# Weight row ends issued by the GpSimd queue in transfers of 8 x 4 rows, with values three groups behind the keys

## The chip, the cores and the metric

The kernel runs on one core of a Trainium2 chip. The metric is the device time of one execution in microseconds. Eleven executions of the kernel before lie between 195.41 and 195.97 us, 0.3% apart, so differences of one per cent are read from several rounds, in which the kernel in question and the kernel before run in turn on the same chip. A profile is one execution. Its span is shorter than the device time (198.4 us for an execution of 200.14 us).

## The reference, cut to what matters

It is one decode step: eight batch rows of attention over a cached window of 1024 positions, and a small MLP, mixed by a gate.

```python
B, Sq, D = 8, 1, 448; Hq, Hkv, Sk, Dh = 16, 8, 4096, 256; F = 1792
q = (x @ wq)                      # wq: 448 x 4096
k, v = last 1024 positions of the caches, 8 kv heads, 8 batches
o = softmax(q k^T / 16) v
a = o @ wo                        # wo: 4096 x 448
b = gelu(layernorm(x) @ w1 + b1) @ w2 + b2     # w1: 448 x 1792
out = g * a + (1 - g) * b         # g = sigmoid(x . gate_w)
```

Keys and values of the window are 67 MB in bf16, the weights 10.6 MB. All of it is read once. The width 448 is 3 x 128 + 64, so `wq` and `w1` have 64 rows left over after three full sets of 128 partitions. These 64 rows are the "row ends" of this document.

## The kernel before

Everything large goes through a ring of nine slots of 128 partitions x 16 KB, filled in a fixed order by one queue, SP (SyncE). One load of a key or value group (four heads of one batch) is 2 MB: 16 KB for each of 128 partitions.

```python
wq_m = A_wq[0:DM, :].rearrange("(p r) n -> p (r n)", r=NR)     # DM = 384, NR = 3
wq_t = A_wq[DM:D, :].rearrange("r (h n) -> (r h) n", h=2)      # 64 rows as 128 half rows
w1_t = B_w1[DM:D, :].rearrange("r (h n) -> (r h) n", h=2)
...
add_kv("k", A_k_cache, 0, parts=2)
add(("w1",), rows_loader([w1_m, w1_t]))
add(("wq", 0), rows_loader([wq_m[:, 0 : 2 * HD]]))
add(("wq", 1), rows_loader([wq_m[:, 2 * HD : 3 * HD], wq_t]))
add(("w2",), rows_loader([w2_v]))
for u in range(1, NQ - 1):                 # NQ = 16 groups
    add_kv("k", A_k_cache, u)
    if u < NQ - 2:
        add_kv("v", A_v_cache, u - 1)
add_kv("k", A_k_cache, NQ - 1)
for u in range(NQ - 3, NQ):
    add_kv("v", A_v_cache, u)
... then wo, in pieces of 896, 896, 896, 448, 224 and 224 KB
```

Each row end is split in two halves, so that all 128 partitions take the same share. The price is a second set of transposed activations and some more matmuls. At the end, values 14 and 15 and the output projection follow the last keys:

```python
u = NQ - 1
transpose_keys(u, steps(u - 1)); scores(u); top(u)
values(u - 2); finish(u - 2)
expo(u); turn(u); bring(u)
values(u - 1); ...; finish(u - 1)
spread_rows(0, HALF); values(u); finish(u); project(0); ...
```

## Time and profile before

| | before |
|---|---|
| time, median (range) of three executions | 195.52 us (195.46 to 195.59) |
| span of the profile | 193.7 us |
| read from HBM | 77.68 MB |
| rate while loading | about 425 GB/s |
| last matmul ends | 190.43 us |
| last weight piece landed | 189.82 us |

From the page of the kernel before: the busy share of the 16 DMA engines in 40 slices of 4.84 us (9 is 90% or more), what they moved in each slice, and two of the queues with packets, MB and share of the engines' time.

```profile
DMA  5999999999999999999999999999999999999950
GB/s 203 397 437 415 430 431 428 426 426 416 420 423 430 426 426 423 430 430 423 425 423 423 430 423 416 428 430 420 426 426 430 420 433 420 423 433 404 414 217 10
...
q1 hardware_dynamic: 6512, 77.67, 95.3%
q8 instruction: 18, 0.29, 0.6%
```

The load runs from the second slice to the 38th without a gap. From the same page, the chain of work that ended last:

```profile
DMA 82%; PE 9%; ACT 3%; DVE 2%; issue 1%; SPq 1%; ACTq 0%
```

The engines are named as the profiler names them: PE is TensorE (matmuls; PEld are its weight loads), DVE is VectorE, ACT is ScalarE, POOL is GpSimd. "SPq" and "ACTq" are the queues of SyncE and ScalarE. Two neighbouring pieces of the same chain, in order of time (start, duration, what):

```profile
120.98 39.72 DMA slot<-in_A_k_cache_dram
...
160.74 0.64 PE ktp L322 x8
```

So the kernel is bound by the load until 160.7 us, when key group 14 has landed. From there a compute chain is the last one. The end of it in the timeline of the kernel before (start, duration, engine, line, operation, output and inputs, count):

```profile
187.11 0.92 PE L563 MATMUL A_ps<-slot,oP 128*8 128x112 bf16 x32
...
187.97 2.46 PE L563 MATMUL A_ps<-slot,oP 128*8 128x112 bf16 x96
...
190.48 0.33 DVE L580 SCALAR_TENSOR_TENSOR res<-A_ps,gg_s,mixb 128x112 bf16<-128x112 f32 x1 [1.92 <-PE A_ps L563]
```

The 96 matmuls run without a wait for the load. But the load ends only about half a microsecond before them (0.6 us by the table, 0.4 us on the clock of the views), so both have to shorten for the time to fall.

One more reading is needed. For each transfer of the bulk load the trace keeps 16 semaphore increments, which I read as one for each of the 16 DMA engines, when its part has landed. They do not name the engine, but the distances to the first repeat from transfer to transfer (15 of the 16 in the two transfers below, within 0.01 us), so each can be followed. Two transfers of the kernel before: time of the first landing, then the distance of all 16 to it, in us.

```
43.69 | 0.00 0.06 0.07 0.10 0.13 0.14 0.18 0.39 0.48 0.62 0.64 0.92 1.07 1.75 1.93 2.01
48.59 | 0.00 0.06 0.07 0.10 0.13 0.14 0.17 0.39 0.48 0.62 0.64 1.07 1.75 1.93 2.02 2.48
last transfer:
184.96 | 0.00 0.08 0.17 0.40 0.49 0.62 0.83 2.04 3.17 3.20 3.22 3.49 3.56 3.75 4.02 4.86
```

Between the first two rows the engine at 0.92 went to 2.48, and no other moved. At 44.72 a packet of 16 KB of the instruction queue ran for 1.02 us. By my matching, the others between 18 and 186 us go with such steps in the same way: each sets one engine back by about 1.55 us, and eight engines take turns. The packets do not name their engine, so this is a reading of the landings. At the end eight engines are late, and the slowest of them ends the load: it lands 2.7 us after the mean of the 16 (187.08).

### The profile page before, as it was taken

What the parts mean: (1) busy time and instruction counts of PE and PEld (TensorE: products, weight loads), DVE (VectorE), ACT (ScalarE), POOL (GpSimd) and SP (SyncE); (2) the same over time, 40 slices, a digit from 0 to 9 for tenths busy, and PEclk for the clock granted to TensorE, in tenths of its full rate; (3) what the DMA queues carried; (4) which work ended last, traced back from release to release, by engine and by line L of the source; (5) the groups of instructions that cost most, each with busy time, mean ns of one, the idle gap of its engine ahead of it and who ended that gap; (6) DMA issues with size and microseconds to landing.
All of it is one profiled execution on the core that took longest, in us unless ns stands there. A gap on an engine that the chain in (4) does not pass through costs nothing.

```text
span 193.7 us, 5200 instructions
## 1 busy us (share of the span) xinstructions
PE 148.1 (76%) x2334; PEld 110.3 (57%) x2334; DVE 112.9 (58%) x259; ACT 82.7 (43%) x101; POOL 0.8 (0%) x7
## 2 busy tenths in 40 slices
PE   1399967777778787878778787878868787984883
PEld 0399936555464646465637373737464646662672
DVE  7532344757475757584847575757565757786320
ACT  2352004536272728181808282828273636582000
POOL 1000000000000000000000000000000000000000
PEclk9998559999999999999999999999999999999555
DMA  5999999999999999999999999999999999999950
GB/s 203 397 437 415 430 431 428 426 426 416 420 423 430 426 426 423 430 430 423 425 423 423 430 423 416 428 430 420 426 426 430 420 433 420 423 433 404 414 217 10
DMA packets 6744, 78.02 MB, mean 403 GB/s; under 512 B 945, under 2 KB 1346, under 8 KB 1986
## 3 DMA queue, kind: packets, MB, share of 16 engines
q1 hardware_dynamic: 6512, 77.67, 95.3%
q8 instruction: 18, 0.29, 0.6%
q10 hardware_dynamic: 210, 0.02, 0.1%
q14 instruction: 4, 0.03, 0.0%
HBM read 77.68 MB, written 0.01 MB: 401 GB/s over the span
## 4 chain that ended last, share of the span: by engine, by line
DMA 82%; PE 9%; ACT 3%; DVE 2%; issue 1%; SPq 1%; ACTq 0%
DMA slot<-in_A_k_cache_dram 77%; DMA slot<-in_B_w_dram 5%; ACT kt L325 2%; PE S_ps L360 2%; PE ktp L322 2%; PE PO L420 2%; PE A_ps L563 2%; ACT E L380 1%; PE sm L437 1%; SPq L107 1%; DVE EB L388 1%; DVE nmx L372 1%; PE sm L399 0%; PE sm L396 0%; PE pp L547 0%
## 5 line engine op out<-in xcount | busy, mean ns | idle before, releaser
L325 ACT COPY kt<-ktp 128x1024 bf16<-128x1024 bf16 x64 | 63.2, 1017 | 82.2 <-PE ktp L322 82.2
L322 PE MATMUL ktp<-ident,slot 128*128 128x128 bf16 x1024 | 70.2, 224 | 22.1 <-ACT kt L325 11.4
L322 PEld LDWEIGHTS <-slot 128*128 128x128 bf16 x1024 | 63.7, 102 | 29.0 <-issue 15.7
L327 DVE COPY kt<-ktp 128x1024 bf16<-128x1024 bf16 x64 | 41.3, 685 | 15.8 <-PE ktp L322 15.6
L372 DVE TENSOR_REDUCE nmx<-S_ps 128x1 f32<-128x1024 f32 x16 | 19.6, 1225 | 22.3 <-PE S_ps L360 22.3
L360 PE MATMUL S_ps<-kt,qw 128*8 128x512 bf16 x256 | 32.3, 627 | 0.3 <-DVE qw L351 0.3
L388 DVE STREAM_TRANSPOSE EB<-E 128x1024 bf16<-128x1024 bf16 x16 | 19.9, 1245 | 6.7 <-ACT E L380 6.5
L420 PE MATMUL PO<-slot,ET 128*8 128x256 bf16 x512 | 18.5, 290 | 6.4 <-DVE ET L401 6.4
L380 ACT ACTIVATE E<-S_ps,nmx 128x1024 bf16<-128x1024 f32 x16 | 17.9, 1120 | 2.4 <-DVE nmx L373 2.4
L420 PEld LDWEIGHTS <-ET 128*8 128x8 bf16 x512 | 12.2, 90 | 10.5 <-DVE ET L401 8.7
L360 PEld LDWEIGHTS <-qw 128*8 128x8 bf16 x256 | 7.3, 95 | 12.0 <-issue 10.4
L401 DVE CAST ET<-sm 128x256 bf16<-128x256 f32 x16 | 6.7, 417 | 0.7 <-PE sm L399 0.7
L396 PE MATMUL sm<-EB,perm 128*128 128x256 bf16 x16 | 4.5, 280 | 1.6 <-DVE EB L388 1.6
L399 PE MATMUL sm<-selr,ones_f 128*128 128x8 f32 x32 | 5.5, 244 | 0.0
L440 DVE CAST oT<-sm 128x16 bf16<-128x16 f32 x16 | 3.5, 221 | 2.8 <-PE sm L437 2.8
L399 PEld LDWEIGHTS sm<-selr,ones_f 128*128 128x128 f32 x32 | 5.0, 196 | 0.1
L339 PE MATMUL qt<-xT,slot 128*128 128x8 bf16 x128 | 3.6, 168 | 0.4 <-DVE z L470 0.4
L339 PEld LDWEIGHTS <-slot 128*128 128x128 bf16 x128 | 3.6, 104 | 0.4 <-issue 0.3
L470 DVE TENSOR_TENSOR z<-hT,b_sb 128x112 f32<-128x112 f32 x1 | 0.3, 275 | 5.3 <-PE hT L460 5.3
L563 PE MATMUL A_ps<-slot,oP 128*8 128x112 bf16 x128 | 3.3, 294 | 0.0
L380 ACT ACTIVATION_READ_ACCUMULATOR E<-S_ps,nmx 128x1 f32 x16 | 3.2, 202 | 0.0
L403 DVE RECIPROCAL rb<-sm 128x8 f32<-128x8 f32 x16 | 3.2, 199 | 0.0
(122 smaller groups left out, 72.2 us busy)
## 6 DMA issues: line engine op xcount, KB each, us to landing
slot<-in_A_v_cache_dram SPq DMA_DIRECT2D x16, 2048.0 KB, 39.3
slot<-in_A_k_cache_dram SPq DMA_DIRECT2D x15, 2048.0 KB, 39.6
slot<-in_A_wo_dram SPq DMA_DIRECT2D x3, 896.0 KB, 32.0
slot<-in_A_k_cache_dram SPq DMA_DIRECT2D x2, 1024.0 KB, 7.2
slot<-in_A_wq_dram SPq DMA_DIRECT2D x1, 2048.0 KB
slot<-in_B_w_dram SPq DMA_DIRECT2D x1, 1568.0 KB
slot<-in_B_w_dram SPq DMA_DIRECT2D x1, 1344.0 KB, 10.1
slot<-in_A_wq_dram SPq DMA_DIRECT2D x1, 1024.0 KB
```

The costliest lines, as they stand in the source:

```text
L322: nc.tensor.transpose(ktp[:, c, :], kn[:, o : o + P], ident[:])
L325: nc.scalar.copy(dst, ktp[:])
L327: nc.vector.tensor_copy(dst, ktp[:])
L339: nc.tensor.matmul(qt[:, k, :], lhsT=w[:, o + c : o + c + P], rhs=xT[:, r + half, :], start=(r == 0 and k == 0), stop=(r == NR), skip_grou ...
L360: nc.tensor.matmul(S_ps[32 * a : 32 * a + RQ, hf * CH * SK : (hf + 1) * CH * SK], lhsT=qw[:, j, b, half, a, :], rhs=KT[hf][:, j, :, a::QUA ...
L372: nc.vector.reduce_max(nmx[:], S_ps[:], axis=AXIS.X, negate=True)
L380: nc.scalar.activation(E[:], S_ps[:], ACT.Exp, bias=nmx[:], scale=1.0, accum_out=rowsum[:])
L388: nc.vector.transpose(EB[:].rearrange("p c r -> p (c r)"), E[:])
L399: nc.tensor.matmul(sm[:, NCK, :], lhsT=ones_f[:], rhs=selr[:], start=True, stop=True)
L401: nc.vector.tensor_copy(ET[:], sm[:, 0:NCK, :])
L420: nc.tensor.matmul(PO[32 * t : 32 * t + RQ, :], lhsT=ET[:, c, 0:RQ], rhs=vn[:, c * Dh : (c + 1) * Dh], start=(c < QUAD), stop=(c >= NCK - ...
L563: nc.tensor.matmul(dst, lhsT=oP[:, j, q, :], rhs=w[:, o + cols.start : o + cols.stop], start=(q == 0 and j == 0), stop=(q == NHQ - 1 and j ...
```

## The change

The intent, as the diff shows it: the row ends are loaded as 64 full rows on partitions 64 to 127, by the GpSimd queue, so that the SP queue does not carry them, and one set of transposed activations for the row ends is enough in place of two (in the MLP, 14 matmuls for them in place of 28). Each transfer is shaped as 8 x 4 rows. Small dummy transfers ("side") stand between them: 14 rows ahead of the first, eight ahead of each other one, ten after the last. I took them to be there to pick the eight engines that work on the row ends. Values are loaded and used three groups after their keys (before: one).

```diff
+    LAG = 3
+    ER = P - DT                                  # 64
...
+    def step_over(n):
+        ...
+        nc.gpsimd.dma_start(side[0:n, ...], A_wq[0:n, 0:32]...)    # n rows of 64 bytes
+    def ends(t, o, src):
+        n = src.shape[1]
+        for h in range(DT // 32):
+            rows = src[DM + 32 * h : DM + 32 * h + 32, :]
+            step_over(NB if turns[0] else 14)    # NB = 8
+            nc.gpsimd.dma_start(
+                t[ER + 32 * h : ER + 32 * h + 32, o : o + n],
+                rows.rearrange("(j i) n -> i j n", i=NB),
+            )
+            if turns[0] == 4:
+                step_over(10)
...
-    add(("w1",), rows_loader([w1_m, w1_t]))
+    add(("w1",), rows_loader([w1_m], B_w1))      # the second argument goes to ends()
...
-    for u in range(1, NQ - 1):
+    for u in range(1, NQ):
         add_kv("k", A_k_cache, u)
-        if u < NQ - 2:
-            add_kv("v", A_v_cache, u - 1)
+        if u >= LAG:
+            add_kv("v", A_v_cache, u - LAG)
...
-                    lhsT=w[:, o + c : o + c + P],
-                    rhs=xT[:, r + half, :],
+                    lhsT=w[p0:P, c : c + P],     # p0 = 64 for the row ends
+                    rhs=xT[p0:P, r, :],
```

(Cut: the same for `w1`, the pools that hold softmax results longer, the identity matrix built ahead of the loads, and the loop of the values.)

More of the change, by code (lines that the diff above doesn't have):

```diff
@@ L51 @@
     NF = F // P
-    FH = F // 2
-    HH = HD // 2
     QUAD = 4
@@ L76 @@
     ktpool = ctx.enter_context(tc.tile_pool(name="ktpool", bufs=4))
-    epool = ctx.enter_context(tc.tile_pool(name="epool", bufs=3))
+    epool = ctx.enter_context(tc.tile_pool(name="epool", bufs=2))
+    opool = ctx.enter_context(tc.tile_pool(name="opool", bufs=LAG + 1))
     ps_s = ctx.enter_context(tc.tile_pool(name="ps_s", bufs=1, space=PSUM))
@@ L111, in kv_loader, with rows_loader @@
         return load
-    def rows_loader(pieces):
+    side = consts.tile([16, 10, 32], BF16)
+    turns = [0]
+    def step_over(n):
+        i = turns[0]
+        turns[0] += 1
+        nc.gpsimd.dma_start(
+            side[0:n, 2 * i : 2 * i + 2, 0:16],
+            A_wq[0:n, 0:32].rearrange("b (a n) -> b a n", a=2),
+        )
[4 more added lines that the diff above has]
+            step_over(NB if turns[0] else 14)
+            nc.gpsimd.dma_start(
+                t[ER + 32 * h : ER + 32 * h + 32, o : o + n],
+                rows.rearrange("(j i) n -> i j n", i=NB),
+            )
+            if turns[0] == 4:
+                step_over(10)
+    def rows_loader(pieces, tail=None):
         def load(t):
@@ L124, in load @@
                 o += n
+            if tail is not None:
+                ends(t, o, tail)
         return load
@@ L137 @@
     wq_m = A_wq[0:DM, :].rearrange("(p r) n -> p (r n)", r=NR)
-    wq_t = A_wq[DM:D, :].rearrange("r (h n) -> (r h) n", h=2)
     w1_m = B_w1[0:DM, :].rearrange("(p r) f -> p (r f)", r=NR)
-    w1_t = B_w1[DM:D, :].rearrange("r (h n) -> (r h) n", h=2)
     w2_v = B_w2.rearrange("(p c) n -> p (c n)", c=NF)
@@ L144 @@
     add_kv("k", A_k_cache, 0, parts=2)
-    add(("w1",), rows_loader([w1_m, w1_t]))
+    add(("w1",), rows_loader([w1_m], B_w1))
     add(("wq", 0), rows_loader([wq_m[:, 0 : 2 * HD]]))
-    add(("wq", 1), rows_loader([wq_m[:, 2 * HD : 3 * HD], wq_t]))
+    add(("wq", 1), rows_loader([wq_m[:, 2 * HD : 3 * HD]], A_wq))
     add(("w2",), rows_loader([w2_v]))
-    for u in range(1, NQ - 1):
+    for u in range(1, NQ):
         add_kv("k", A_k_cache, u)
-        if u < NQ - 2:
-            add_kv("v", A_v_cache, u - 1)
-    add_kv("k", A_k_cache, NQ - 1)
-    for u in range(NQ - 3, NQ):
+        if u >= LAG:
+            add_kv("v", A_v_cache, u - LAG)
+    for u in range(NQ - LAG, NQ):
         add_kv("v", A_v_cache, u)
@@ L171 @@
     x_sb = consts.tile([NB, D], BF16)
+    ident = consts.tile([P, P], BF16)
+    make_identity(nc, ident[:])
     pump()
@@ L181 @@
     nc.scalar.dma_start(b1_sb[:], B_b1.rearrange("(p c) -> p c", c=NF))
-    ident = consts.tile([P, P], BF16)
-    make_identity(nc, ident[:])
     ones_f = consts.tile([P, P], F32)
@@ L191 @@
     nc.vector.memset(PO[:], 0.0)
-    NX = NR + 2
+    NX = NR + 1
     DQ = D // QUAD
@@ L200, in quads @@
         ]
-    xz = consts.tile([NB, 2, P], BF16)
-    yz = consts.tile([NB, 2, P], BF16)
+    xz = consts.tile([NB, P], BF16)
+    yz = consts.tile([NB, P], BF16)
     nc.vector.memset(xz[:], 0.0)
@@ L223, in transposed, with ends_of @@
             nc.tensor.transpose(tp[:, r, :], src[:, r:DM:NR], ident[:NB, :NB])
-        for h in range(2):
-            nc.tensor.transpose(tp[:, NR + h, :], srcz[:, h, :], ident[:NB, :NB])
+        nc.tensor.transpose(tp[:, NR, :], srcz[:], ident[:NB, :NB])
         nc.vector.tensor_copy(dst[:], tp[:])
-    for h in range(2):
-        nc.vector.tensor_copy(xz[:, h, h::2], x_sb[:, DM:D])
+    def ends_of(dst, src):
+        nc.vector.tensor_copy(
+            dst[:, ER:P].rearrange("b (h i j) -> b h i j", h=DT // 32, i=NB),
+            src[:, DM:D].rearrange("b (h j i) -> b h i j", h=DT // 32, i=NB),
+        )
+    ends_of(xz, x_sb)
     transposed(xT, x_sb, xz)
@@ L270, in norm_and_gate @@
         )
-        for h in range(2):
-            nc.vector.tensor_copy(yz[:, h, h::2], y_sb[:, DM:D])
+        ends_of(yz, y_sb)
         transposed(yT, y_sb, yz)
@@ L335, in query @@
             w, o = slot("wq", r // 2), (r % 2) * HD
+            p0 = ER if r == NR else 0
             for k in range(Hq * NJ):
-                col = (k // NJ) * Dh + (k % NJ) * P
-                half, c = divmod(col, HH) if r == NR else (0, col)
+                c = o + (k // NJ) * Dh + (k % NJ) * P
                 nc.tensor.matmul(
                     qt[:, k, :],
-                    lhsT=w[:, o + c : o + c + P],
-                    rhs=xT[:, r + half, :],
+                    lhsT=w[p0:P, c : c + P],
+                    rhs=xT[p0:P, r, :],
                     start=(r == 0 and k == 0),
@@ L399, in bring @@
         nc.tensor.matmul(sm[:, NCK, :], lhsT=ones_f[:], rhs=selr[:], start=True, stop=True)
-        ET = epool.tile([P, NCK, RQ], BF16, tag="ET", name="ET")
+        ET = opool.tile([P, NCK, RQ], BF16, tag="ET", name="ET")
         nc.vector.tensor_copy(ET[:], sm[:, 0:NCK, :])
@@ L403, in bring @@
         nc.vector.reciprocal(rb[:], sm[:, NCK, :])
-        rsel = epool.tile([P, RQ], F32, tag="rsel", name="rsel")
+        rsel = opool.tile([P, RQ], F32, tag="rsel", name="rsel")
         nc.vector.tensor_tensor(rsel[:], rb[:], sel[:], op=ALU.mult)
@@ L457, in mlp_hidden @@
                 )
-        for h in range(2):
-            for c in range(NF):
-                nc.tensor.matmul(
-                    hT[64 * h : 64 * h + 64, c, :],
-                    lhsT=w[:, NR * F + c : NR * F + FH : NF],
-                    rhs=yT[:, NR + h, :],
-                    start=False,
-                    stop=True,
-                    skip_group_check=True,
-                )
+        for c in range(NF):
+            nc.tensor.matmul(
+                hT[:, c, :],
+                lhsT=w[ER:P, NR * F + c : NR * F + F : NF],
+                rhs=yT[ER:P, NR, :],
+                start=False,
+                stop=True,
+                skip_group_check=True,
+            )
         done()
@@ L518 @@
     mlp_out(hs)
-    for u in range(1, NQ - 1):
+    for u in range(1, NQ):
         transpose_keys(u, steps(u - 1))
-        if u < NQ - 2:
-            values(u - 1)
+        if u >= LAG:
+            values(u - LAG)
         scores(u)
         top(u)
-        if u < NQ - 2:
-            finish(u - 1)
+        if u >= LAG:
+            finish(u - LAG)
     u = NQ - 1
-    transpose_keys(u, steps(u - 1))
-    scores(u)
-    top(u)
+    expo(u)
+    turn(u)
     values(u - 2)
     finish(u - 2)
-    expo(u)
-    turn(u)
     bring(u)
@@ L574 @@
     finish(u)
-    project(0)
     spread_rows(HALF, NHQ)
-    for q in range(1, NHQ):
+    for q in range(NHQ):
         project(q)
```

## The prediction

> **What bounds the kernel now.** The bulk load. The page shows 77.68 MB read at about 425 GB/s, the DMA row at nine tenths nearly throughout. In the chain of waits 82% is DMA, up to the landing of key group 14 (160.7 us). Then a compute chain binds: keys 14 and 15 are transposed back to back (160.7 to 175.1), softmax of 15, values 14, values 15, output projection; its last matmul ends at 190.43. The trace's semaphore increments of the last weight transfer land from 184.96 to 189.82, so both must shorten.
>
> **The 16 DMA engines do not end together.** In the last transfer seven land within 0.83 us, one 2.04 us behind the first, seven 3.2 to 4.0, one 4.9. The mean is 187.08. Following the gaps back, each 16 KB packet of the instruction queue (18 of them, about 10 us apart, 1.1 us each) sets one engine back by 1.55 us; the pattern fits eight engines in turn, two hits each, one three.
>
> **What the change does.**
> 1. Values trail keys by three groups: key 15 lands one 2 MB load (4.9 us) earlier and key 14 two, so no back-to-back transposes wait behind the last keys. Compute is then done with the values near 185, with slack. The end becomes: last weight piece lands, eight matmuls (about 0.2 us), mix 0.33 us, output as before. Alone this gains about 0.4 us.
> 2. The 64 row ends (229 KB and 524 KB) leave the SP queue, where every engine carries 47 KB of them. Each GpSimd transfer has a source of outer size 8[...]. These get 94 KB, the others none: plus and minus 47 KB, 1.77 us at 16 KB per 0.614 us. No run here shows which eight, nor whether the upper partitions slow anyone.
> 3. Fewer MLP matmuls (1.5 us), and the GpSimd issues, are early, off the critical path; the nine slots stay ahead.
>
> **Sum.** If the eight are those that fetch no instructions: fetch engines end 1.4 to 3.1 us after today's first, the others 1.8 to 3.8, last landing near 188.7 in place of 189.8; with slack in compute about 1.3 us saved. If the groups half overlap: nothing. If they coincide: last landing 191.6, 1.5 us lost. The first seems likelier: the step of six looks chosen. Even perfect balance (187.1) saves only 3 us, 1.6%.
>
> Predicted **194.2 us**, range 192.8 to 196.4. Chances: faster by over 2% 0.04, within 2% 0.93, slower by over 2% 0.03.
>
> **What would show it.** Step 1: key 15's transposes start near 160; the chain of waits is DMA up to the last weight piece, with only a few matmuls after it. Step 2: a queue of its own with 0.75 MB; the spread of the last landings falls from 4.9 to about 2 us (right) or grows to 6 (wrong). Step 3: no gap in the DMA row.
>
> **What would make it wrong.** Another engine group than assumed;[...] a late third instruction fetch on the last engine; GpSimd descriptors so slow that the ring starves.

"These" in step 2 are the eight engines to which, by my assumption, all four transfers go; "the step of six" is the first dummy of 14 rows less the eight of the next. The sum is 195.5 us less about 1.3, that is 194.2.

## More of the kernel before

For the comparison later, the view of engines by time window of the kernel before. The columns are: window, length, busy time and instruction count of PE, PE weight loads, DVE, ACT and POOL, granted TensorE clock, DMA share, GB/s. The last column is the one to read.

```profile
core 0: us, PE busy (x) PEld busy (x) DVE busy (x) ACT busy (x) POOL busy (x), PEclk, DMA share, GB/s
5.00:10.00 5.00, 1.99 (x17) 1.85 (x18) 2.53 (x14) 1.78 (x3) 0.00 (x0) 1.00 1.00 403
10.00:15.00 5.00, 5.00 (x49) 5.00 (x47) 2.04 (x3) 2.94 (x3) 0.00 (x0) 1.00 1.04 437
15.00:20.00 5.00, 5.00 (x72) 4.89 (x71) 0.73 (x2) 1.01 (x1) 0.00 (x0) 0.84 0.97 405
20.00:25.00 5.00, 4.63 (x138) 4.56 (x137) 1.54 (x6) 0.30 (x1) 0.00 (x0) 0.50 1.04 435
25.00:35.00 10.00, 6.70 (x128) 4.58 (x128) 5.07 (x15) 3.19 (x5) 0.00 (x0) 0.82 1.02 428
```

## The result, and the profile after

| | before | after |
|---|---|---|
| time, median (range) of four executions | 195.56 us (195.46 to 195.59) | 200.26 us (199.88 to 200.68) |
| ratio, 95% interval | | 1.0243 (1.0228 to 1.0258) |
| mean landing of the last weight piece | 187.08 | 191.3 |
| last landing of it | 189.82 | 194.35 |

Ratios here and below are the mean time of one kernel's runs over that of the other's of the same rounds, so not quite the ratio of the medians quoted. Landing times of different runs are placed on the span's clock by the first bulk packet, which is good to about 0.2 us. In the views of the chain, which take their zero from the first instruction, the same landings stand about 0.2 us later (194.56 for the 194.35 of this table); differences between kernels are not touched by it.

The changed kernel is 2.4% slower. The page of the changed kernel, in the same rows (slices of 4.96 us):

```profile
DMA  5999999999999999999999999999999999999950
GB/s 206 342 317 332 326 435 432 418 423 426 420 426 426 430 426 426 420 430 421 423 423 426 430 426 423 418 433 420 436 420 426 420 426 423 430 418 419 400 202 11
...
q1 hardware_dynamic: 6224, 76.91, 93.9%
q0 software_dynamic: 416, 0.76, 1.4%
q8 instruction: 18, 0.29, 0.6%
```

The DMA row has not changed at all: nines throughout. The rate has: slices two to five move 317 to 342 GB/s in place of 397 to 437. Busy engines that move less have longer packets (611 and 934 ns, below). The windows of the changed kernel put an end to the slow stretch:

```profile
5.00:10.00 5.00, 2.21 (x19) 2.06 (x20) 2.21 (x13) 2.01 (x4) 1.86 (x4) 1.00 1.05 349
10.00:15.00 5.00, 4.20 (x54) 3.81 (x51) 2.76 (x4) 3.26 (x4) 0.00 (x0) 1.00 1.02 318
15.00:20.00 5.00, 3.57 (x56) 3.51 (x56) 0.00 (x0) 0.46 (x1) 0.00 (x0) 0.86 0.99 329
20.00:25.00 5.00, 0.39 (x14) 0.35 (x14) 1.54 (x6) 0.30 (x1) 0.00 (x0) 0.50 1.00 326
25.00:35.00 10.00, 7.06 (x198) 4.98 (x194) 2.75 (x12) 0.00 (x0) 0.00 (x0) 0.64 1.01 427
```

From 5 to 25 us the kernel before moved 8.40 MB (5 us times the sum of its four rates), the changed one 6.61 MB. The 1.79 MB that are missing take 4.2 us at 427 GB/s. That is the shift of the mean landing, and nearly all of the 4.7 us. The slow stretch is the time in which the row ends are under way: packets of the GpSimd queue run from about 6 to 23 us.

The end of the chain of waits of the changed kernel (start, duration, what):

```profile
136.56 39.15 DMA slot<-in_A_v_cache_dram
175.74 18.82 DMA slot<-in_A_wo_dram
194.56 0.04 issue
194.60 0.38 PE A_ps L585 x8
194.98 0.02 issue
195.01 0.33 DVE res L601
```

So the lag did what it was meant to do. The compute chain is gone from the end: the last weight piece lands, eight matmuls follow, then the mix. But the load ends later by more than that.

Packets tell it most directly. Of the bulk packets of 16 KB that start between 11 and 16 us, the median took 611 ns before (longest 646) and 934 ns after (shortest 652). Not one of them ran at the usual speed, though there were never more than eight packets of row ends in flight.

### The profile page after: what moved, and what is told of

It is laid out like the page before. It is cut to its first block, busy times and chain, and to the rows that moved or that the text cites. A ratio compares the mean times of both kernels' runs of the same rounds, so it can differ in the third digit from the quotient of the medians.

```text
span 198.4 us, 5181 instructions
## 1 busy us (share of the span) xinstructions
PE 147.1 (74%) x2318; PEld 109.1 (55%) x2318; DVE 112.2 (57%) x257; ACT 82.9 (42%) x101; POOL 6.0 (3%) x16
## 4 chain that ended last, share of the span: by engine, by line
DMA 86%; PE 8%; ACT 3%; issue 0%; SPq 0%; DVE 0%; ACTq 0%
DMA slot<-in_A_k_cache_dram 57%; DMA slot<-in_A_v_cache_dram 20%; DMA slot<-in_A_wo_dram 9%; PE ktp L348 5%; PE S_ps L386 2%; ACT kt L351 2%; ACT E L406 1%; PE PO L446 1%; PE sm L425 0%; PE A_ps L585 0%; DVE res L601 0%; PE sm L422 0%; SPq L147 0%; SPq L108 0%; ACTq L351 0%
## 5 line engine op out<-in xcount | busy, mean ns | idle before, releaser
L348 PE MATMUL ktp<-ident,slot 128*128 128x128 bf16 x1024 | 71.4, 226 | 22.3 <-DMA slot<-in_A_k_cache_dram 11.0
L348 PEld LDWEIGHTS <-slot 128*128 128x128 bf16 x1024 | 65.4, 103 | 29.3 <-issue 15.6
L365 PE MATMUL qt<-xT,slot 128*128 128x8 bf16 (+1 forms) x128 | 3.8, 167 | 5.1 <-DMA slot<-in_A_wq_dram 5.1
L365 PEld LDWEIGHTS <-slot 128*128 128x128 bf16 (+1 forms) x128 | 3.6, 103 | 5.3 <-DMA slot<-in_A_wq_dram 5.2
L585 PE MATMUL A_ps<-slot,oP 128*8 128x112 bf16 x128 | 3.9, 291 | 1.6 <-DMA slot<-in_A_wo_dram 1.6
L377 DVE TENSOR_SCALAR qw<-qt 128x32 bf16<-128x32 f32 x8 | 0.9, 181 | 6.9 <-PE qt L365 6.9
L585 PEld LDWEIGHTS <-oP 128*8 128x8 bf16 x128 | 2.9, 116 | 2.4 <-issue 2.4
L476 PE MATMUL hT<-yT,slot 128*128 128x8 bf16 x42 | 2.7, 202 | 2.0 <-DMA slot<-in_B_w_dram 2.0
```

The source lines that it names most:

```text
L348: nc.tensor.transpose(ktp[:, c, :], kn[:, o : o + P], ident[:])
L365: nc.tensor.matmul(qt[:, k, :], lhsT=w[p0:P, c : c + P], rhs=xT[p0:P, r, :], start=(r == 0 and k == 0), stop=(r == NR), skip_group_check=True,
L585: nc.tensor.matmul(dst, lhsT=oP[:, j, q, :], rhs=w[:, o + cols.start : o + cols.stop], start=(q == 0 and j == 0), stop=(q == NHQ - 1 and j ...
```

## The experiments

Theory A: the loss depends on which eight engines load the row ends and to which partitions they write, the two taken together, and for some pairs there is none. The expectations below also rested on an assumption of which pairings are good. The trace names neither the engine of a packet nor its partitions, so that is not shown. What can be tested is the effect of the partitions with all else the same (e4 with e5, e9 with e10), and of the first dummy with the partitions the same (the changed kernel with e9). Rivals: the lag; the GpSimd queue or a second queue as such (B); the order of the source rows; eight engines fed twice, wherever they write (C).

All experiments keep the lag and gave correct results. "Slices" are those of the page, "the first piece of `wo`" is the 896 KB transfer that follows value group 15.

### e1: the lag alone

```diff
 the kernel before, with
-            add_kv("v", A_v_cache, u - 1)
+        if u >= LAG:
+            add_kv("v", A_v_cache, u - LAG)      # and the compute loop to match
```

> The kernel before with the values three groups behind the keys, and nothing else of the change. Both theories: the load rate stays at 410 to 440 GB/s in every slice after the first, so the lag costs nothing; the chain of waits becomes DMA up to the last weight piece. Expected 195.1 us (194.6 to 195.6). A rival that blames the lag for the loss (keys ahead of values starve or stall the ring early) expects about 200 us and slices two to five at 320 to 340 GB/s, as in the changed kernel.

195.56 us against 195.44, ratio 1.0014 (0.9994 to 1.0035). Slices two to five are 388, 434, 408, 441 GB/s. The end of the chain of waits of e1:

```profile
131.40 39.15 DMA slot<-in_A_v_cache_dram
170.57 20.24 DMA slot<-in_A_wo_dram
190.81 0.04 issue
190.85 0.38 PE A_ps L561 x8
```

The lag costs nothing that can be told from noise, and moves the end from the compute chain to the load. It does not gain the 0.4 us either. In this profile the last landing was at 190.6 in place of 189.8, with the same mean (187.12 against 187.08). By the landings, the instruction packet at about 181.4 us set back an engine that was already the latest. But the profiled execution was the slowest of e1's four (196.24 us, the others 195.37 to 195.74), so why those three gain nothing either is not shown.

### e2 and e3: the other half of the partitions, and another first dummy

```diff
 e2, the changed kernel with
-    ER = P - DT
+    ER = 0                     # row ends on partitions 0 to 63
 e3, the changed kernel with
-            step_over(NB if turns[0] else 14)
+            step_over(NB if turns[0] else 6)
-                step_over(10)
+                step_over(2)
```

> The changed kernel with the row ends on partitions 0 to 63 in place of 64 to 127; same GpSimd transfers[...]. Theory A[...]:[...] slices two to five return to 410 GB/s or more and the time to 194 to 196 us; the landings of the first 25 us no longer split into two eights more than 4 us apart. Theory B (transfers by the GpSimd queue, or their source rows, slow everything wherever they land): 200 us again, slices two to five at 320 to 340 GB/s.

> The changed kernel with the first dummy over 6 rows and the last over 2 (14 and 10 before)[...]. Theory A:[...] slices two to five at 410 GB/s or more, 193 to 196 us. Theory B: 200 us, slices two to five at 320 to 340 GB/s, whatever the group.

e2: 198.83 us, ratio 1.0172 (1.0156 to 1.0187), slices 390, 352, 344, 378. e3: 201.14 us, ratio 1.0305 (1.0283 to 1.0326), slices 352, 335, 338, 358. Both missed theory A's numbers, which rested on a guess of mine about the engines that the dummies pick. Either theory A was wrong or the guess was. The order of the two partition halves did matter (e2 is 1.4 us faster than the changed kernel), which B does not explain.

### e4 and e5: the same on the ACT queue

```diff
 e4, the changed kernel with
-            step_over(NB if turns[0] else 14)
-            nc.gpsimd.dma_start(
+            nc.scalar.dma_start(
 e5 = e4 with ER = 0
```

> The changed kernel with the four row-end transfers issued by the ACT queue in place of the GpSimd queue, without dummies: same sources, same upper partitions, eight engines each. Theory A[...]:[...] 199 to 201 us and slices two to five at 320 to 340 GB/s. Theory B in its form that blames the GpSimd queue itself: 194 to 196 us and slices at 410 or more.

> The row ends by the ACT queue (as in e4), on partitions 0 to 63.[...] Theory A[...]:[...] slices two to five at 400 GB/s or more and 194 to 197 us (the eight engines carry 94 KB more and end later). Theory B (something that does not depend on the partitions: source rows, eight engines alternating between two queues): 199 to 201 us as e4.

The two kernels differ in the partitions alone. The landings of e4 come in eights, as those of the changed kernel do (eight within 1.0 us, the other eight 5.1 us later or more, in the transfer that began to land at 18.6 us). I read that as eight engines at work; which eight, no trace says. e4: 200.81 us, ratio 1.0278 (1.0261 to 1.0296). e5: 196.96 us, ratio 1.0074 (1.0056 to 1.0091). The windows of e4, then of e5:

```profile
5.00:10.00 5.00, 0.00 (x0) 0.00 (x0) 0.00 (x0) 0.00 (x0) 0.00 (x0) 1.00 1.07 341
10.00:15.00 5.00, 0.00 (x0) 0.00 (x0) 0.00 (x0) 0.00 (x0) 0.00 (x0) 1.00 1.00 299
```

```profile
5.00:10.00 5.00, 0.00 (x0) 0.00 (x0) 0.00 (x0) 0.00 (x0) 0.00 (x0) 1.00 1.02 421
10.00:15.00 5.00, 0.00 (x0) 0.00 (x0) 0.00 (x0) 0.00 (x0) 0.00 (x0) 1.00 1.04 442
15.00:20.00 5.00, 0.42 (x4) 0.25 (x4) 2.85 (x15) 2.04 (x3) 0.00 (x0) 1.00 0.80 333
20.00:25.00 5.00, 3.37 (x30) 3.22 (x31) 2.02 (x10) 2.04 (x3) 0.00 (x0) 1.00 0.86 337
```

Same queue, same transfers, same source rows: with the row ends written to partitions 0 to 63 the load runs at 421 and 442 GB/s, to partitions 64 to 127 at 341 and 299. The GpSimd queue is not needed for the loss. These two kernels have a flaw of their own: the row ends stand ahead of the small input `x` in the ACT queue, so PE and ACT do nothing before 15 us, and the SP queue waits for a `wq` landing (13.1 us in its view of waits in e5) before it issues more. The DMA share of 0.80 and 0.86 in e5 after 15 us is that starvation, and no slow packets: the median bulk packet of 16 KB between 11 and 16 us took 611 ns. It is the likely reason why e5 is not as fast as e1; no run without the flaw was made.

### e6, e7, e8: other shapes of the transfers

```diff
 e6, as e4 with the source rows in plain order
-                rows.rearrange("(j i) n -> i j n", i=NB),
+                rows.rearrange("(i j) n -> i j n", i=NB),
 e7, the changed kernel with one transfer of 64 rows, no dummies
+        nc.gpsimd.dma_start(t[ER:P, o : o + n], src[DM:D, :])
 e8, e1 with its half rows on 128 partitions issued by GpSimd
-                nc.sync.dma_start(dst, ap)
+                eng = nc.gpsimd if any(ap is x for x in tails) else nc.sync
+                eng.dma_start(dst, ap)
```

> As e4 (ACT queue, upper partitions, eight engines), but each engine reads four neighbouring rows in place of every eighth row. Theory B in the form that blames the order of the source rows: 195 to 197 us and slices two to five at 400 GB/s. Theory A and every other form: 200 to 201 us, as e4, slices two to five at 290 to 340 GB/s.

> The row ends by the GpSimd queue to the same 64 upper partitions, but as one transfer of 64 rows each,[...] without dummies. Theory A:[...] the loss is smaller but there: 196 to 199 us. If eight engines alternating between queues is the cause (not the partitions): 195 to 196 us. If the 64 full rows themselves are slow to read: 199 to 201 us.

> The kernel with the lag (e1), whose row ends stay 128 half rows on all partitions as in the kernel before, but are issued by the GpSimd queue.[...] theory A expects no loss against e1, 195 to 196 us and slices two to five at 400 GB/s or more. If the mere presence of a second queue beside the bulk load costs the time: 198 to 200 us.

e6 did not test what it was made for. In plain order the 32 rows of a transfer follow each other, and the landings no longer split into two eights (16 of them within 0.94 us at 20 us): apparently 16 engines took two rows each (an estimate, 32 rows over 16 landings). It gave 198.59 us, ratio 1.0161 (1.0137 to 1.0185). The order of the source rows is thus not separated by it. e7: 199.21 us, ratio 1.0184 (1.0162 to 1.0205), just above its range. The loss is still there, as in e6 with its 16 landings together, so it is not a matter of eight engines alone. Its time also lies in the range of the third case of its expectation, that 64 full rows are slow to read. e9 and e12 below read the same rows and have no slow stretch, so that case falls. e8: 196.21 us, ratio 1.0032 (1.0013 to 1.0051), 406 to 440 GB/s in windows of 5 us from 5 to 25 us. The half rows on all 128 partitions, issued by the GpSimd queue, cost 0.3%: the queue as such is cleared.

### e9, e10, e11: a first dummy of eight rows, and of ten

```diff
 e9, the changed kernel with
-            step_over(NB if turns[0] else 14)
+            step_over(NB)              # and no step_over(10)
 e10 = e9 with ER = 0
 e11, the changed kernel with first dummy 10 and last 14
```

> The changed kernel with a first dummy of 8 rows (14 before) and no last one[...]. In the changed kernel and in e3[...] all packets were slow while the row ends ran. Theory A[...] the loss goes: slices two to five at 410 GB/s or more, 193.0 to 195.5 us, or up to 197 if these eight also fetch the instructions. Theory C (eight engines fed by the GpSimd queue slow the load wherever they write): 199 to 201 us.

> As e9, but the row ends on partitions 0 to 63:[...] same queue, same rows. Theory A:[...] 199 to 202 us, slices two to five at 320 to 350 GB/s. Theory C: no difference from e9.

> The changed kernel with[...] (first dummy 10 rows, last 14). Theory A:[...] 198 to 201 us and slices two to five under 370 GB/s[...]. Theory C: as e9.

e9: 197.58 us, ratio 1.0101 (1.0086 to 1.0116). e10: 201.58 us, ratio 1.0317 (1.0293 to 1.0341). e11: 199.3 us, a single execution of unknown state; slices 396, 344, 362, 399, so its time is in the range expected, and two of its four slices are above the 370 expected. The windows of e9, then of e10:

```profile
5.00:10.00 5.00, 2.07 (x18) 1.92 (x19) 2.35 (x13) 1.87 (x4) 1.30 (x3) 1.00 1.00 389
10.00:15.00 5.00, 4.79 (x69) 4.58 (x67) 2.77 (x4) 3.40 (x4) 0.00 (x0) 1.00 1.02 418
15.00:20.00 5.00, 2.80 (x46) 2.70 (x44) 1.54 (x6) 0.75 (x2) 0.00 (x0) 0.85 1.00 416
20.00:25.00 5.00, 2.66 (x93) 2.58 (x94) 0.00 (x0) 0.00 (x0) 0.00 (x0) 0.50 1.02 430
```

```profile
5.00:10.00 5.00, 2.07 (x18) 1.91 (x19) 2.35 (x13) 1.87 (x4) 1.30 (x3) 1.00 1.04 357
10.00:15.00 5.00, 4.29 (x55) 3.90 (x53) 2.77 (x4) 3.32 (x4) 0.00 (x0) 1.00 1.03 319
15.00:20.00 5.00, 3.43 (x56) 3.42 (x56) 0.00 (x0) 0.54 (x1) 0.00 (x0) 0.87 0.97 326
20.00:25.00 5.00, 0.19 (x4) 0.10 (x2) 1.54 (x6) 0.30 (x1) 0.00 (x0) 0.50 1.01 317
```

e9 differs from the changed kernel in the first dummy (8 rows for 14) and in nothing that is as large, and the slow stretch is gone. e10 has e9's dummies and the other partitions, and the slow stretch is back (317 to 326 GB/s from 10 to 25 us, where e9 has 416 to 430). So with the partitions the same the first dummy switches it, and with the dummies the same the partitions do, as theory A says. Theory C falls.

The runs in between are graded, which the two pairs alone do not show. The median bulk packets (16 KB, 11 to 16 us), with the row ends on partitions 64 to 127: 611 ns with a first dummy of 8 rows (e9), 796 with 10 (e11), 880 with 6 (e3), 934 with 14 (the changed kernel). On partitions 0 to 63: 611 ns with none (e12), 814 with 14 (e2), 954 with 8 (e10). What sets the degree is open: the engine of a packet is in no trace.

e9 is still 1% slower than the kernel before, and just above its range. Its rate has recovered, so the reason is another one, and the landings show it. The first piece of `wo` in e9:

```
176.99 | 0.00 0.65 0.67 0.72 1.24 2.45 3.20 3.32 3.38 3.61 6.34 6.37 6.43 6.44 6.50 6.56
```

By my following of the landings, the eight engines of the group lag by 3.2 us from the start, which is about the 94 KB of row ends that they carry (3.5 us at 16 KB per 614 ns). Six of them were also hit by two instruction packets each (3.1 us more): these are at 6.3 to 6.6. The mean landing is 180.6, as in the kernel before (180.3), but the last is at 183.6 in place of 182.3, and a further instruction packet then hit one of the late engines.

### e12: no dummy ahead of the first transfer, lower partitions

```diff
 the changed kernel with ER = 0 and
-            step_over(NB if turns[0] else 14)
...
-            if turns[0] == 4:
-                step_over(10)
+            step_over(NB)              # after each transfer, none ahead of the first
```

> The row ends by the GpSimd queue on partitions 0 to 63, with no dummy ahead of the first transfer (one of 8 rows after each)[...]. Theory A: no slow packets, slices two to five at 400 GB/s or more.[...] two engines carry both the row ends and the fetches, where e9 had six: the landings of the late transfers have two engines near 6.5 us behind the first, and the rest within 4.7. Expected 196.2 us (195.6 to 197.0), so still not better than the kernel before. If theory A is wrong[...], 199 us or more.

("Two engines" rested on the six late ones of e9, and on the assumption, not shown, that e12 loads its row ends with the other eight.)

195.96 us, ratio 1.0018 (1.0001 to 1.0034). The windows of e12 show 405, 419, 400 and 439 GB/s from 5 to 25 us. In the landings of the first piece of `wo`, two engines are at 5.92 and 5.95 us and all others within 4.9:

```
177.33 | 0.00 0.31 2.77 2.83 2.84 2.87 2.96 2.98 3.04 3.18 3.21 3.41 3.74 4.82 5.92 5.95
```

The range for the time and the count of late engines were met (their lag was 5.9 us where 6.5 was expected). With no dummy ahead of the first transfer and the row ends on partitions 0 to 63, the whole loss of the change is gone but for a few tenths (195.96 us against 195.63 for the kernel before in the same rounds).

### e13: row ends in transfers of 24, 24 and 16 rows

The prediction had hoped for a gain from balance. To look for it, the row ends were cut into transfers of 24, 24 and 16 rows, shaped as 6 x 4, 6 x 4 and 4 x 4, with zeros in the partitions between, which are multiplied too. That six engines carry the 48 rows and four the 16, and that the six are without instruction packets, was assumed.

```diff
+    SEGS = ((0, 0, 6), (32, 24, 6), (64, 48, 4))     # partition, first row, rows / 4
+        nc.vector.memset(t[:, o : o + n], 0.0)
+        for (p, r0, e), over in zip(SEGS, (10, 2, 4)):
+            rows = src[DM + r0 : DM + r0 + 4 * e, :]
+            nc.gpsimd.dma_start(t[p : p + 4 * e, o : o + n],
+                                rows.rearrange("(j i) n -> i j n", i=e))
+            step_over(over)
```

> The row ends by the GpSimd queue, 24 and 24 rows[...] (partitions 0 to 23 and 32 to 55) and 16 rows[...] (partitions 64 to 79)[...], with zeros in the unused partitions.[...] they get 94 KB of row ends (3.5 us at 16 KB per 0.614 us), which is what a fetching engine loses (two times 1.55 us). Four engines get 47 KB as in the kernel before, two of them at least beside fetches; the other six none. If the prediction's balance term holds: the late transfers land within 5 us of the first (5.9 in e12), the last about 1.0 us earlier against their mean than in the kernel before, and the time is 194.6 us (194.0 to 195.3), faster than both kernels. If it does not hold (other costs of the second queue, or other engines fetch): 195.6 to 196.5.

("They" in the expectation are the six engines assumed for the 48 rows.)

195.60 us against 195.48, ratio 1.0003 (0.9991 to 1.0015). The rate is as in the kernel before (407 to 433 GB/s in windows of 5 us from 5 to 35 us). The time missed the 194.0 to 195.3 us for the case that the balance pays, and lies in the range for the case that it does not. But one engine landed 6.8 us after the first and another 5.3. So two engines of the loaded group probably had instruction packets after all. My reading of which engines fetch was right in number for e12, and wrong here. Whether the set depends on the program, or one engine was misread, is open.

### All of it in one table

Mean and last landing of the first piece of `wo`, and the median duration of row-end packets of 8 KB (wq) where there are at least 30.

| kernel | row ends as issued | partitions | mean landing | last | 8 KB packet | ratio |
|---|---|---|---|---|---|---|
| before | 128 half rows | all | 180.3 | 182.3 | | 1 |
| e1 | 128 half rows | all | 180.4 | 183.9 | | 1.0014 |
| e8, GpSimd | 128 half rows | all | 180.2 | 183.2 | | 1.0032 |
| e13 | 24, 24, 16 rows | 0 to 23, 32 to 55, 64 to 79 | 180.1 | 183.5 | 312 ns | 1.0003 |
| e9 | first dummy 8 | 64 to 127 | 180.6 | 183.6 | 309 ns | 1.0101 |
| e12 | no first dummy | 0 to 63 | 180.5 | 183.3 | 309 ns | 1.0018 |
| e5, ACT | no dummies | 0 to 63 | 181.8 (starved) | 183.4 | 309 ns | 1.0074 |
| e11 | first dummy 10 | 64 to 127 | 182.6 | 185.6 | 340 ns | (one run, 199.3 us) |
| e2 | first dummy 14 | 0 to 63 | 183.0 | 186.2 | 313 ns | 1.0172 |
| e6, ACT | 8 x 4 rows in plain order | 64 to 127 | 183.0 | 184.6 | 502 ns | 1.0161 |
| e7, GpSimd | one transfer of 64 rows | 64 to 127 | 183.5 | 185.0 | 615 ns | 1.0184 |
| e3 | first dummy 6 | 64 to 127 | 183.6 | 186.9 | 407 ns | 1.0305 |
| after | first dummy 14 | 64 to 127 | 184.5 | 187.5 | 440 ns | 1.0243 |
| e10 | first dummy 8 | 0 to 63 | 184.5 | 187.8 | 420 ns | 1.0317 |
| e4, ACT | no dummies | 64 to 127 | 185.7 | 187.4 | 383 ns | 1.0278 |

Of the kernels with transfers of 8 x 4 rows (e6, in plain order, aside), the three without slow packets (e9, e12, e5) have 8 KB packets of 309 ns. The three with the latest mean landing (after, e10, e4), 4 us or more after the kernel before, have packets of 383 to 440 ns. e2, e3 and e11 stand between them in mean landing. In e2 most row ends themselves are quick (313 ns), and it is the bulk packets that are slow.

## Why the prediction was wrong, point by point

- **What bounds the kernel: right.** Load and compute ended together; after the change only the load does.
- **Step 1, the lag: right in mechanism, its gain too large.** The chain of waits became DMA up to the last weight piece, and eight matmuls of 0.38 us (predicted about 0.2) follow. The gain of 0.4 us (a ratio of 0.998) did not show: e1 measured 1.0014 (0.9994 to 1.0035).
- **Step 2, the row ends: this step failed.** The prediction costed them as "plus and minus 47 KB, 1.77 us at 16 KB per 0.614 us". It took the usual packet speed for granted, for the bulk load and for the row ends. In the changed kernel bulk packets of 16 KB took 934 ns (median, 11 to 16 us), and the mean landing went up by 4.2 us. The prediction said that no run showed "whether the upper partitions slow anyone", and put nothing for it into the sum or the range. e4 with e5, and e9 with e10, show that the choice of partitions alone, with queue, dummies and source rows the same, switches it on and off (299 and 442 GB/s, and 418 and 319, from 10 to 15 us).
- **The group.** Its rule for the engines that the dummies pick is not shown by any trace. What the runs show is that the first dummy matters: on partitions 64 to 127 the bulk packets took 611 ns with 8 rows, and 796, 880 and 934 with 10, 6 and 14. That the step of six "looks chosen" for the engines without instruction packets was a guess about intent. By the landings of the changed kernel's last transfer (two engines within 0.3 us of the first, eleven at 3.1 to 4.5 us, three at 5.6 to 6.7) I read that it did leave most of the fetching engines without row ends. The spread of the last landings was nevertheless 6.7 us, past the 6 that the prediction had given for its wrong case.
- **The gain from balance (1.3 us): not seen in any run.** e12 and e13 have no slow stretch, and still a spread of 5.9 and 6.7 us and ratios of 1.0018 and 1.0003. So the balance that the sum counted on did not pay even where the packets kept their speed.
- **Step 3: right, and of no help.** There was no gap in the DMA row. It stayed at nine while the packets took half as long again.
- **The range.** Its upper end (196.4) allowed for imbalance alone. The only case costed above the time before was one of 1.5 us.

What stays open is why all 16 engines slow down. In the changed kernel never more than eight packets of row ends were in flight, yet no engine was far ahead: in the transfer that began to land at 18.6 us the first eight landed within 1.0 us, the other eight 5.1 us later or more, and of the bulk packets that start between 11 and 16 us none took less than 652 ns. No run shows the cause.

## What to carry to other kernels

A partial load beside a full one can slow the full one, by where it writes: here the same row ends by the same queue, on the other 64 partitions, took the load from 418 to 319 GB/s (e9 and e10, 10 to 15 us). So before trusting a new placement, compare the packet times and the GB/s row, since the DMA busy row stays at nine tenths either way. Look also at the spread of the landings: here the last engine ended the load 2.7 us after the mean, and that is the most a rebalancing could have saved of the load; none of the runs here saved it. To test such a placement, vary the rows of the first dummy, and the partitions, each alone, as the changed kernel, e9 and e10 do.
